# The routed token's feed-forward gets earlier keys in a planned order, and the planner's clock gets new times

## The chip, the cores and the metric

The kernel runs on one core of one Trainium2 chip. The metric is the device time of one execution in microseconds (us). TensorE is called PE here, VectorE DVE, ScalarE ACT, GpSimd POOL, and the engine whose queue issues every DMA is SP.

## The reference, cut to what matters

The kernel mixes two layers over the same 2048 tokens of 640 features: an attention with a compressive memory (32 heads of 20, four segments of 512 tokens), and a feed-forward for one routed token.

```python
g = _sigmoid((x * gate_w).sum(-1, keepdims=True))
# a: attention with memory, one segment of 512 tokens after the other
for s in range(N):
    p = _softmax(qs @ ks.T * scale + mask)
    a_dot = p @ vs
    a_mem = (phi(qs) @ M) / (phi(qs) @ z + 1e-6)
    o = sigmoid(beta) * a_mem + (1 - sigmoid(beta)) * a_dot
    M = M + phi(ks).T @ vs ; z = z + phi(ks).sum()
a = o @ wo
# b: x, plus the feed-forward at the token with the highest score r
r = x @ w_r
idx = argmax(r)
y = (silu(x[idx] @ w_gate) * (x[idx] @ w_up)) @ w_down * sigmoid(r[idx])
b = x.at[idx].add(y)
out = g * a + (1 - g) * b
```

## The kernel before

**How the order comes about.** The program does not issue its instructions as it writes them. Every piece of work is first entered into a plan with an engine (PE, ACT, DVE, POOL, SP), a duration in the planner's own clock, a key, and the buffers it reads and writes. `Plan.order` then plays the plan through: at each step it takes the engine whose best piece can start first, and among the pieces of that engine that can start at once (within 0.03 us) the one with the smallest key. The order that comes out is issued as it stands, and on the chip each engine works through its part in that order. A duration in the plan therefore never makes an instruction longer or shorter; it only decides what stands ahead of what. A DMA is two things in the plan: its issue on SP (0.36 us), and its landing, for which the planner adds 0.65 us, a time on 16 modelled rings, and 0.4 us.

**Keys.** The attention works in 32 groups `n` (4 heads of one segment). Group `n` has its score steps with row maxima under keys `n-1` to `n` (`a_step`, L792 and L798, the maxima at L804), its exponentials under `n` to `n+1` (`b_step`, L840 and L845), and its product with the values under `n+1` (`pv_step`, L866). One unit of the key is thus one group of heads. Projections of the next segment half (`paired`, L611, 64-row pairs) have keys around them, and so have the writes (L748) and reads (L729) of the memory.

**Modes on PE.** Pieces in mode "C" (L866, L729, L748 and the feed-forward, L967) use the array in 32-column strips; all others are in mode "R". The planner charges `SWITCH` for a change. A piece that is lazy (memory and feed-forward) is taken in mode C if its key is at most 1.0 above the smallest, and out of mode R only when its key is 1.0 behind all others that can start.

**The router and the feed-forward.** `route` (key 14.0) finds the token: `to_row` writes 128 maxima of 4 bytes each to DRAM (`rrow<-best`), reads them back as one row (`jp<-rrow`) and takes their maximum on DVE (L907); `to_all` sends it to all partitions (`sel<-top`, `all<-sel`). This is done twice, and then SP loads the token's row (`xrow`). The feed-forward has 18 up steps (`up_step`, keys 16.02 + 0.5 i), an activation (`ffn_act`, 25.0), 8 down steps (`down_step`, 25.6 + 0.3 i) and an end (`ffn_end`, 28.0), which leaves `yb`, the token's result on all partitions (POOL, L1025). A step loads one or two weight tiles into a ring of two (`ffn`), so the loads of the next step wait for the matmuls of this one.

**The output.** `o_job` makes one of 16 output tiles of 128 tokens: x is loaded, scaled (ACT, L1069), `yb` is added (DVE, L1070), 10 groups of six matmuls with `wo` follow (L611, 64x320), then L1081 adds the two and a DMA stores the tile. Twelve tiles (segments 0 to 2) have keys from 28.95 on and use three x buffers in the memory of `kk`; the last four have keys from 33.6. A PSUM pair is opened for a tile only when the work that its evacuation needs has been started in the plan:

```python
ps.guard = [d for u in ps.users if u.eng != "PE" for d in u.deps
            if d not in ps.users and d.eng != "PE"]
```

For an output tile this list holds L1070, and so the tile's matmuls stand behind `yb` in PE's order.

Of the kernel before, what the change touches and what calls it, by code (L numbers as in the profile page):

```python
# [112 lines left out]
class Plan:  # L113


    SWITCH = 0.2
    ISSUE = 0.36

    def __init__(self):
# [63 lines left out]
    def order(self):  # L183
# [86 lines left out]
        while len(done) < total:  # L270
            for e in stale:
                cur[e] = choose(e)
            stale = set()
            pick = None
            for e in ENGINES:
                c = cur[e]
                if c is not None and (pick is None or c[0] < pick[0]):
                    pick = c
            if pick is None:
                raise RuntimeError("the order is stuck: " + "; ".join(  # L280
                    f"{e}: {[(round(t.key, 2), t.seq, t.mode) for t in avail[e]][:6]}" for e in ENGINES))
            est, t = pick
            e = t.eng
            avail[e].remove(t)
            t.start = est
            know = seen[e]
            for d in t.deps:
                if d.eng != "PE":
                    know = max(know, d.seen)
                elif e != "PE":  # L290
                    know = max(know, d.index)
            if t.fence is not None:
                before, poke = t.fence
# [12 lines left out]
            t.fin = est + dur
            if t.desc is not None:
                count, size, wide = t.desc
                each = -(-count // wide) * (0.008 + size / 23400.0)
                begin, t.fin = t.fin + 0.65, 0.0  # L310
                for i in range(wide):
                    rings[i] = max(rings[i], begin) + each
                    t.fin = max(t.fin, rings[i] + 0.4)
            stale.add(e)
            if t.opens is not None:
                ps = t.opens
                if ps.need == 2:
# [40 lines left out]
def tile_infini_mod(  # L358
# [37 lines left out]

    banks = [psum.tile([128, 2, 512], F32, name=f"bank{i}") for i in range(PAIRS)]

    def dma(key, dst, src, reads, writes, desc, wide=16, issue=Plan.ISSUE):
        plan.add("SP", issue, lambda: nc.sync.dma_start(dst, src), key, reads, writes, desc=(*desc, wide))  # L400

    def dve(key, dur, fn, reads, writes):
        plan.add("DVE", dur, fn, key, reads, writes)
# [13 lines left out]
    def dves(n):  # L417
        return 0.13 + n / 940.0
# [7 lines left out]
    def split(key, engine, hi, lo, src, n, reads, hpart, lpart, more=0.0):  # L426

        act(key, acts(n) + 0.4 * more, lambda: nc.scalar.copy(hi, src), reads, [hpart])  # L428
        e, dur = (nc.gpsimd, pools(n) + 0.4 * more) if engine == "POOL" else (nc.vector, dves(n) + more)
        plan.add(engine, dur, lambda: e.tensor_tensor(out=lo, in0=src, in1=f32(hi), op=OP.subtract), key,  # L430
                 [*reads, hpart], [lpart])

# [288 lines left out]
    def memory_read(u, g, key):  # L721
# [7 lines left out]
                nc.tensor.matmul(t[32 * j:32 * j + 32, ps.bank, :], mbd.t[:, g, 32 * j:32 * j + 32], e.t, start=True, stop=True)  # L729
        pe(key, 0.9, fn, [(mbd, g), e], [ps], mode="C", opens=ps, lazy=True)  # L730
        nts[n] = nt = nt_ring.take()
        dve(key, dves(L), lambda: nc.vector.transpose(nt.t[:, 1, :], banks[ps.pair][:, ps.bank, :]), [ps], [(nt, 1)])
        z = sub(nt.t, L + DH, [[32, 16]])
        pool(key, 0.26, lambda: nc.gpsimd.tensor_scalar(z, z, 1e-6, None, op0=OP.add), [(nt, 1)], [(nt, 1)])

# [44 lines left out]
    def a_step(n, p, t, key):  # L780
# [7 lines left out]
        def fn():  # L788
# [6 lines left out]
            for w, other in ((tri, 0), (irt, 1)):  # L795
                for b in range(2):
                    dst = sub(a, 512 * b + at_ + 64 * (b ^ other), [[128, d], [1, 64]])
                    nc.tensor.matmul(dst, w.t[64 * b:64 * b + 64, :], sub(id64.t[64 * b:64 * b + 64], 0, [[0, d], [1, 64]]),  # L798
                                     start=False, stop=True, skip_group_check=True)
        dur = sum(stream(w) for _, _, w in blocks) + 2 * max(0.065, 0.03 * diag[1] + 0.01)  # L800
        pe(key, dur, fn, [(q, 0), (q, 1), (k, 0), (k, 1), tri, irt, id64], [ps], opens=ps)
        m_ = mxs[n]
        for i, at_, w in blocks:
# [48 lines left out]
    def pv_step(n, key):  # L852
# [14 lines left out]
                                     pt[j % 2, min(c, 2)].t[:, j // 2, at_:at_ + w], start=c == 0, stop=c == 3)  # L867
        pe(key, 2.2, fn, [*pt.values(), v], [ps], mode="C", opens=ps)
        nt = nts.pop(n) if n in nts else nt_ring.take()
        dve(key, dves(L), lambda: nc.vector.transpose(nt.t[:, 0, :], banks[ps.pair][:, ps.bank, :]), [ps], [(nt, 0)])  # L870
        norm(n, nt, key)

    def norm(n, nt, key):
# [10 lines left out]
        rd, rm = (sub(z.t, 16 * a, [[1, 16], [0, DH]]) for a in range(2))  # L884
        dve(key, dves(16 * DH), lambda: nc.vector.tensor_tensor(out=dot, in0=dot, in1=rd, op=OP.mult), [(nt, 0), z], [(nt, 0)])
        if s:
            pool(key, 1.15, lambda: nc.gpsimd.tensor_tensor(out=mem, in0=mem, in1=rm, op=OP.mult), [(nt, 1), z], [(nt, 1)])  # L887
            dve(key, 0.6, lambda: nc.vector.tensor_tensor(out=dot, in0=dot, in1=mem, op=OP.add), [(nt, 0), (nt, 1)], [(nt, 0)])
        dve(key, dves(L), lambda: nc.vector.transpose(o.t, nt.t[:, 0, :]), [(nt, 0)], [o])
        h = HH * hf + 4 * g  # L890
        dma(key, oT[32 * h:32 * h + 128, L * s:L * s + L], o.t, [o], [oTb[n]], (128, 2048))

# [7 lines left out]
    NT = S // 128  # L900

    def to_row(col, reads, k, key):
        dma(key, rrow[k].t.rearrange("o p -> p o"), col, reads, [rrow[k]], (128, 4))
        t = row
        dma(key, t.t, rrow[k].t, [rrow[k]], [t], (1, 512))
        m = buf(f"top{k}", [1, 1])
        dve(key, 0.25, lambda: nc.vector.tensor_reduce(out=m.t, in_=t.t, axis=AX.X, op=OP.max), [t], [m])  # L907
        return m

    def to_all(m, k, key):  # L910
        dma(key, sel[k].t, m.t, [m], [sel[k]], (1, 4))
        t = buf(f"all{k}", [128, 1])
        dma(key, t.t, bass.AP(tensor=sel[k].t.tensor, offset=sel[k].t.offset, ap=[[0, 128], [1, 1]]), [sel[k]], [t], (128, 4))
        return t

    def route():
# [25 lines left out]
        def load():  # L942
            i = nc.sync.value_load(ix.t[0:1, 0:1], min_val=0, max_val=S - 1)
            nc.sync.dma_start(xr.t, x[bass.ds(i, 1), :].rearrange("o (p t) -> (o p) t", t=KT))
        plan.add("SP", 1.2, load, key, [ix], [xr], desc=(128, 20, 16))
        R.update(gx=gx, gb=gb, oh=oh, sg=sg, xr=xr)

    at(14.0, route)
# [28 lines left out]
    def up_step(i):  # L977
# [2 lines left out]
        w = (wg, wu)[m].rearrange("(p t) f -> t p f", t=KT)  # L980
        parts = [(w[t, :, FP * f3:FP * f3 + FP], 128, [R["xr"]], lambda t=t: R["xr"].t[:, t:t + 1])
                 for t in range(2 * tt, min(2 * tt + 2, KT))]
        ffn_step(16.02 + 0.5 * i, fgu, FF // 4 * m + 144 * f3, 144, parts, tt == 0)

    for i in range(18):
        at(16.02 + 0.5 * i, lambda i=i: up_step(i))

    ht = buf("ht", [108, 2, 16])
    hv = buf("hv", [108, 16])

    def ffn_act():
# [11 lines left out]
        dve(key, 0.2, lambda: nc.vector.tensor_tensor(out=hv.t, in0=hv.t, in1=g_, op=OP.mult), [hv, (ht, 0)], [hv])  # L1003
        dve(key, 0.2, lambda: nc.vector.tensor_tensor(out=hv.t, in0=hv.t, in1=u_, op=OP.mult), [hv, (ht, 1)], [hv])

    at(25.0, ffn_act)
    ya = buf("ya", [128, YP])
    yb = Buf(fgu.t[:, :D], fgu)

    def down_step(i):  # L1010
        w = wd.rearrange("(p t) f -> t p f", t=16)
        parts = [(w[t], 108, [hv], lambda t=t: hv.t[:, t:t + 1]) for t in (2 * i, 2 * i + 1)]
        ffn_step(25.6 + 0.3 * i, ya, 0, YP, parts, i == 0)

    for i in range(8):
        at(25.6 + 0.3 * i, lambda i=i: down_step(i))

    def ffn_end():
        key = 28.0
        a = ya.t[0:1, :]  # L1020
        src = bass.AP(tensor=a.tensor, offset=a.offset, ap=[[a.ap[0][0] * 32, 4], [1, YP]])
        d = yrow.t
        dma(key, bass.AP(tensor=d.tensor, offset=d.offset, ap=[[YP, 4], [1, YP]]), src, [ya], [yrow], (4, 640))
        dma(key, yb.t, bass.AP(tensor=d.tensor, offset=d.offset, ap=[[0, 128], [1, D]]), [yrow], [yb], (128, 2560))
        pool(key, 1.5, lambda: nc.gpsimd.tensor_scalar(yb.t, yb.t, R["sg"].t, None, op0=OP.mult), [yb, R["sg"]], [yb])  # L1025

    at(28.0, ffn_end)

# [160 lines left out]
```

## Time and profile before

| | before |
|---|---|
| median of 3 runs | 681.44 us (681.03 to 681.76) |
| the profiled execution, its own time | 678.01 us |
| its span, first to last instruction | 676.3 us |
| mean granted TensorE clock | 0.955 of full speed |
| PE busy | 589.7 us (87%) |
| DVE, ACT, POOL busy | 435.1, 342.6, 295.3 us |
| DMA | 119.49 MB, mean 177 GB/s |

The rows of the trace are of the profiled execution. Its own time is 1.7 us above its span and 3.4 us below the median.

### The profile page before, as it was taken

How to read it: one execution, taken by the hardware profiler on the slowest of the kernel's cores; microseconds unless marked ns; L12 is line 12 of the kernel's file. 1: busy time of each engine (PE TensorE's matmuls, PEld its weight loads, DVE VectorE, ACT ScalarE, POOL GpSimd, SP SyncE). 2: the span in 40 equal slices, each digit the busy share in tenths (PEclk: the TensorE clock that was granted, in tenths of full speed). 3: DMA queues.
4: the chain of work that ended last, by engine and by line, in shares of the span. 5: the costliest groups of instructions: out<-in, count | busy, mean ns of one | idle time of the engine just before them, and what ended most of it. 6: DMA issues, size and time to landing. Idle time of an engine off the chain costs nothing.

```text
span 676.3 us, 18951 instructions
## 1 busy us (share of the span) xinstructions
PE 589.7 (87%) x7760; PEld 437.3 (65%) x7760; DVE 435.1 (64%) x783; ACT 342.6 (51%) x590; POOL 295.3 (44%) x408
## 2 busy tenths in 40 slices
PE   5989998998899867869899999988998787998886
PEld 2777765676667634546678765765676543687886
DVE  6767757776777675356867667666786757554332
ACT  7744764665475544536466655664445751340310
POOL 8953335443654463313633254435343742432310
PEclk9999999999999977979999999999998987799899
DMA  7577564543545444157757666567477554256422
GB/s 259 194 259 245 194 177 156 172 170 122 160 144 187 150 133 127 48 177 257 205 179 224 196 206 214 192 195 212 157 252 243 157 190 135 75 178 210 138 98 79
DMA packets 55943, 119.49 MB, mean 177 GB/s; under 512 B 6994, under 2 KB 10608, under 8 KB 55856
## 3 DMA queue, kind: packets, MB, share of 16 engines
q1 hardware_dynamic: 55856, 118.28, 54.4%
q8 instruction: 61, 1.00, 0.7%
q14 instruction: 26, 0.21, 0.1%
HBM read 72.62 MB, written 45.11 MB: 174 GB/s over the span
## 4 chain that ended last, share of the span: by engine, by line
PE 52%; DVE 18%; DMA 17%; issue 4%; SPq 3%; ACT 3%; POOL 2%; DVEq 0%; ACTq 0%; POOLq 0%
PE bank L611 24%; PE bank L866 10%; DVE mx L804 6%; PE bank L840 5%; PE bank L792 4%; SPq L400 3%; PE bank L729 3%; DMA rrow<-best 2%; DMA qs<-mr 2%; DVE nt L870 2%; DMA ffn<-in_wu_dram 2%; DMA kk<-in_x_dram 2%; PE bank L967 2%; DMA pb<-in_wc_dram 2%; PE bank L798 2%
## 5 line engine op out<-in xcount | busy, mean ns | idle before, releaser
L804 DVE TENSOR_REDUCE mx<-bank 128x2 f32<-128x1024 f32 (+3 forms) x256 | 199.1, 817 | 38.6 <-PE bank L798 35.4
L845 ACT ACTIVATE pb<-bank 128x768 f32<-128x768 f32 x128 | 101.8, 811 | 64.6 <-PE bank L840 49.7
L845 ACT ACTIVATE pa<-bank 128x1024 f32<-128x1024 f32 x64 | 65.7, 1026 | 93.9 <-PE bank L840 71.6
L847 POOL TENSOR_SCALAR_AFFINE_SELECT pb<-pb 128x256 f32<-128x256 f32 (+1 forms) x128 | 72.3, 568 | 88.5 <-ACT pb L845 86.7
L611 PE MATMUL bank<-xhi,whi 64*128 64x512 f32 (+1 forms) x480 | 100.8, 402 | 7.5 <-ACT whi L428 6.3
L792 PE MATMUL bank<-ks,qs 60*128 60x512 f32 (+3 forms) x512 | 79.4, 339 | 24.9 <-DVE mx L804 9.9
L840 PE MATMUL bank<-qs,ks 62*128 62x512 f32 (+3 forms) x512 | 81.0, 369 | 16.1 <-DVE mx L804 5.4
L611 PE MATMUL bank<-xhi,wlo 64*128 64x512 f32 (+1 forms) x480 | 90.9, 361 | 2.1 <-POOL wlo L430 1.1
L430 POOL TENSOR_TENSOR xlo<-raw,xhi 128x512 fp32r<-128x512 f32 x53 | 69.7, 1336 | 48.3 <-ACT xhi L428 29.8
L611 PE MATMUL bank<-xlo,whi 64*128 64x512 f32 (+1 forms) x480 | 90.3, 358 | 0.0
L792 PEld LDWEIGHTS bank<-ks,qs 60*128 60x128 f32 x512 | 49.3, 188 | 38.9 <-DVE mx L804 14.2
L840 PEld LDWEIGHTS bank<-qs,ks 62*128 62x128 f32 x512 | 47.8, 193 | 39.5 <-DVE mx L804 9.1
L870 DVE STREAM_TRANSPOSE nt<-bank 128x512 f32<-128x512 f32 x32 | 22.8, 713 | 67.3 <-PE bank L967 20.5
L430 POOL TENSOR_TENSOR lo<-xs,hi 128x512 fp32r<-128x512 f32 x40 | 52.2, 1321 | 31.3 <-ACT hi L428 19.9
L611 PEld LDWEIGHTS bank<-xhi,whi 64*128 64x128 f32 x480 | 49.8, 191 | 17.7 <-ACT whi L428 6.6
L611 PE MATMUL bank<-whi,xhi 64*128 64x320 f32 x320 | 51.3, 316 | 8.4 <-DVE nil L599 8.4
L611 PE MATMUL bank<-vhi,xhi 64*128 64x322 f32 x320 | 57.5, 339 | 0.6 <-DVE mx L804 0.6
L866 PEld LDWEIGHTS bank<-pb,va 128*32 128x32 f32 x768 | 27.7, 118 | 41.5 <-issue 36.9
L887 POOL TENSOR_TENSOR nt<-nt,zr 128x320 f32<-128x320 f32 x24 | 24.0, 999 | 69.8 <-DVE zr L881 68.9
L611 PEld LDWEIGHTS bank<-xhi,wlo 64*128 64x128 f32 x480 | 49.7, 190 | 6.6 <-POOL wlo L430 2.8
L847 POOL TENSOR_SCALAR_AFFINE_SELECT pa<-pa 128x256 f32<-128x256 f32 x64 | 28.9, 452 | 56.9 <-ACT pa L845 55.4
L611 PEld LDWEIGHTS bank<-xlo,whi 64*128 64x128 f32 x480 | 49.4, 188 | 5.7
(127 smaller groups left out, 1242.8 us busy)
## 6 DMA issues: line engine op xcount, KB each, us to landing
stk<-hi SPq DMA_DIRECT2D x40, 512.0 KB
qs<-stk SPq DMA_DIRECT2D x64, 240.0 KB
ks<-stk SPq DMA_DIRECT2D x64, 240.0 KB
stk<-lo SPq DMA_DIRECT2D x40, 256.0 KB
raw<-in_xT_dram SPq DMA_DIRECT2D x35, 256.0 KB
oT<-on SPq DMA_DIRECT2D x32, 256.0 KB
ffn<-in_wg_dram SPq DMA_DIRECT2D x15, 288.0 KB
ffn<-in_wu_dram SPq DMA_DIRECT2D x15, 288.0 KB
```

The lines of the kernel that those rows point to most:

```text
L400: plan.add("SP", issue, lambda: nc.sync.dma_start(dst, src), key, reads, writes, desc=(*desc, wide))
L430: plan.add(engine, dur, lambda: e.tensor_tensor(out=lo, in0=src, in1=f32(hi), op=OP.subtract), key, [*reads, hpart], [lpart])
L611: nc.tensor.matmul(t[:, b, :n], w[64 * r:64 * r + 64], m[64 * r:64 * r + 64], start=i == 0 and p == 0, stop=ends and p == 2, skip_group_ch ...
L729: nc.tensor.matmul(t[32 * j:32 * j + 32, ps.bank, :], mbd.t[:, g, 32 * j:32 * j + 32], e.t, start=True, stop=True)
L792: nc.tensor.matmul(a[:, b, at_:at_ + w], q.t[64 * b:64 * b + ST, p, 128 * i:128 * i + 128], k.t[64 * b:64 * b + ST, p, :w], start=m == 0, ...
L804: dve(key - 0.6, 0.15 + 2 * w / 960.0, lambda i=i, at_=at_, w=w: nc.vector.tensor_reduce(out=m_.t[:, :, p, i], in_=banks[ps.pair][:, :, at ...
L840: nc.tensor.matmul(bt[:, b, at_:at_ + w], k.t[64 * b:64 * b + ST + 2, p, 128 * c:128 * c + 128], q.t[64 * b:64 * b + ST + 2, p, L - w:], s ...
L845: act(key - 0.4, 0.22 + 2 * w / 1270.0, lambda: nc.scalar.activation(pt.t, banks[ps.pair][:, :, :w], AF.Exp, scale=SCALE), [ps], [pt])
L847: pool(key, 0.42 if t < 2 else 0.64, lambda: nc.gpsimd.affine_select(out=d, in_=d, pattern=[[0, 2], [0, len(cs)], [1, 128]], base=0, chann ...
L866: nc.tensor.matmul(o[32 * j:32 * j + 32, ps.bank, L - w:], v.t[:, c, VW * h:VW * h + 32], pt[j % 2, min(c, 2)].t[:, j // 2, at_:at_ + w], ...
L870: dve(key, dves(L), lambda: nc.vector.transpose(nt.t[:, 0, :], banks[ps.pair][:, ps.bank, :]), [ps], [(nt, 0)])
L887: pool(key, 1.15, lambda: nc.gpsimd.tensor_tensor(out=mem, in0=mem, in1=rm, op=OP.mult), [(nt, 1), z], [(nt, 1)])
```

## The change

All of it is in the plan; no instruction is added, removed or given another shape. The feed-forward's keys become FIRST + UP i for the up steps (15.5 + 0.36 i, so 15.5 to 21.6), 22.0 for the activation, DOWN + 0.25 i for the down steps (22.5 to 24.25), and 24.7 for the end. Landings get an `extra`: 0.8 us for every load that reads only what was there at the start, 6.4 us for the write of the 128 maxima, 1.9 us for their reading back, 1.4 us for the two spreadings to all partitions, and 1.0 us for the token's row. Some durations and the charge for a mode change are set anew.

```diff
+FIRST, UP, DOWN = 15.5, 0.36, 22.5
-    SWITCH = 0.2
+    SWITCH = 0.1
-                count, size, wide = t.desc
+                count, size, wide, extra = t.desc
-                    t.fin = max(t.fin, rings[i] + 0.4)
+                    t.fin = max(t.fin, rings[i] + 0.4 + extra)
-    def dma(key, dst, src, reads, writes, desc, wide=16, issue=Plan.ISSUE):
+    def dma(key, dst, src, reads, writes, desc, wide=16, issue=Plan.ISSUE, extra=0.0):
+        if not reads:
+            extra = 0.8
...
-        e, dur = (nc.gpsimd, pools(n) + 0.4 * more) if engine == "POOL" else (nc.vector, dves(n) + more)
+        e, dur = (nc.gpsimd, pools(n) + 0.4 * more) if engine == "POOL" else (nc.vector, dves(n) + (0.0 if not more else -0.02))
...
-        dur = sum(stream(w) for _, _, w in blocks) + 2 * max(0.065, 0.03 * diag[1] + 0.01)
+        dur = sum(stream(w) for _, _, w in blocks) + 0.07
...
-            pool(key, 1.15, lambda: nc.gpsimd.tensor_tensor(out=mem, in0=mem, in1=rm, op=OP.mult), ...
-            dve(key, 0.6, lambda: nc.vector.tensor_tensor(out=dot, in0=dot, in1=mem, op=OP.add), ...
+            pool(key, 1.04, ...
+            dve(key, 0.49, ...
...
-        dma(key, rrow[k].t.rearrange("o p -> p o"), col, reads, [rrow[k]], (128, 4))
+        dma(key, rrow[k].t.rearrange("o p -> p o"), col, reads, [rrow[k]], (128, 4), extra=6.4)
-        dma(key, t.t, rrow[k].t, [rrow[k]], [t], (1, 512))
+        dma(key, t.t, rrow[k].t, [rrow[k]], [t], (1, 512), extra=1.9)
...
-        ffn_step(16.02 + 0.5 * i, fgu, FF // 4 * m + 144 * f3, 144, parts, tt == 0)
+        ffn_step(FIRST + UP * i, fgu, FF // 4 * m + 144 * f3, 144, parts, tt == 0)
-        key = 25.0
+        key = DOWN - 0.5
-        ffn_step(25.6 + 0.3 * i, ya, 0, YP, parts, i == 0)
+        ffn_step(DOWN + 0.25 * i, ya, 0, YP, parts, i == 0)
-        key = 28.0
+        key = DOWN + 2.2
```

Three transposes on DVE (L732, L870, L889) get 0.71 or 0.72 us for 0.67 us in the plan.

## Rows read from the trace of the kernel before

**Rows 1.** Windows: PE, PEld, DVE, ACT, POOL busy (instructions), PEclk, DMA share, GB/s.

```profile
240.00:300.00 60.00, 42.29 (x362) 26.41 (x358) 31.73 (x72) 24.10 (x57) 19.86 (x31) 0.78 0.35 109
300.00:500.00 200.00, 186.30 (x2694) 135.65 (x2694) 138.40 (x253) 115.07 (x190) 88.22 (x126) 1.00 0.66 206
...
533.00:584.00 51.00, 39.95 (x416) 20.85 (x406) 29.86 (x57) 20.82 (x30) 22.90 (x36) 0.77 0.48 152
584.00:651.00 67.00, 58.60 (x754) 55.19 (x752) 32.76 (x50) 20.40 (x29) 20.39 (x18) 0.97 0.49 162
651.00:676.30 25.30, 19.34 (x252) 18.46 (x252) 6.97 (x15) 2.19 (x4) 2.55 (x2) 0.94 0.18 66
```

**Rows 2.** Chain that ended last: start, us, what.

```profile
255.25 7.58 DMA rrow<-best
...
279.80 8.30 DMA rrow<-best
288.12 3.63 DMA jp<-rrow
...
671.68 0.88 DVE pb L1081
```

**Rows 3.** Timeline of PE, 260 to 294: in brackets idle before, releaser.

```profile
267.18 0.86 PE L792 MATMUL bank<-ks,qs 60*128 60x512 f32 x2 [3.99 <-DVE mx L804]
...
293.03 0.69 PE L792 MATMUL bank<-ks,qs 60*128 60x384 f32 x2 [6.81 <-DVE ix L929]
```

**Rows 4.** Timeline of DVE, 282 to 292.

```profile
291.77 0.27 DVE L907 TENSOR_REDUCE top<-jp 1x1 f32<-1x128 f32 x1 [8.33 <-DMA jp<-rrow]
```

**Rows 5.** Timeline of PE, 305 to 575: feed-forward (L967) and two value products (L866).

```profile
305.82 1.06 PE L866 MATMUL bank<-pa,va 128*32 128x512 f32 x8
...
314.93 0.70 PE L967 MATMUL bank<-ffn,xrow 128*32 128x144 f32 x16
...
478.38 1.06 PE L866 MATMUL bank<-pa,va 128*32 128x512 f32 x8
...
485.17 0.45 PE L967 MATMUL bank<-ffn,xrow 128*32 128x144 f32 x8
...
498.84 0.73 PE L967 MATMUL bank<-ffn,hv 108*32 108x160 f32 x16
...
507.94 0.48 PE L967 MATMUL bank<-ffn,hv 108*32 108x160 f32 x8 [1.59 <-DMA ffn<-in_wd_dram]
...
531.83 0.75 PE L967 MATMUL bank<-ffn,hv 108*32 108x160 f32 x16
...
563.96 0.75 PE L967 MATMUL bank<-ffn,hv 108*32 108x160 f32 x16
...
568.87 1.49 PE L967 MATMUL bank<-ffn,hv 108*32 108x160 f32 x16
...
574.65 1.29 PE L967 MATMUL bank<-ffn,hv 108*32 108x160 f32 x16
```

**Rows 6.** Timeline of PE, 463.9 to 464.6: one step between pairs.

```profile
463.96 0.31 PE L611 MATMUL bank<-vhi,xlo 64*128 64x322 f32 x2
464.20 0.45 PE L967 MATMUL bank<-ffn,xrow 128*32 128x144 f32 x8
464.58 0.41 PE L611 MATMUL bank<-vhi,xhi 64*128 64x322 f32 x2
```

**Rows 7.** Timelines of POOL, DVE and PE, 534 to 585.

```profile
534.12 2.49 POOL L430 TENSOR_TENSOR xlo<-raw,xhi 128x512 fp32r<-128x512 f32 x2
...
581.70 1.89 POOL L1025 TENSOR_SCALAR fgu<-fgu,sg 128x640 f32<-128x640 f32 x1 [2.81 <-DMA fgu<-yrow]
...
583.72 2.60 DVE L1070 SCALAR_TENSOR_TENSOR kk<-fgu,oh,kk 128x640 f32<-128x640 f32 x3
...
584.22 0.34 PE L611 MATMUL bank<-whi,xhi 64*128 64x320 f32 x2
```

**Rows 8.** Waits of SP's queue, 300 to 584: us in total, times, longest.

```profile
SPq L400 <- PE bank L967: 28.0, 19, 4.8
```

More of the change, by code (lines that the diff above doesn't have):

```diff
@@ L397, in tile_infini_mod @@
     banks = [psum.tile([128, 2, 512], F32, name=f"bank{i}") for i in range(PAIRS)]
-    def dma(key, dst, src, reads, writes, desc, wide=16, issue=Plan.ISSUE):
-        plan.add("SP", issue, lambda: nc.sync.dma_start(dst, src), key, reads, writes, desc=(*desc, wide))
+    def dma(key, dst, src, reads, writes, desc, wide=16, issue=Plan.ISSUE, extra=0.0):
+        if not reads:
+            extra = 0.8
+        plan.add("SP", issue, lambda: nc.sync.dma_start(dst, src), key, reads, writes, desc=(*desc, wide, extra))
     def dve(key, dur, fn, reads, writes):
@@ L731, in memory_read @@
         nts[n] = nt = nt_ring.take()
-        dve(key, dves(L), lambda: nc.vector.transpose(nt.t[:, 1, :], banks[ps.pair][:, ps.bank, :]), [ps], [(nt, 1)])
+        dve(key, 0.71, lambda: nc.vector.transpose(nt.t[:, 1, :], banks[ps.pair][:, ps.bank, :]), [ps], [(nt, 1)])
         z = sub(nt.t, L + DH, [[32, 16]])
@@ L869, in pv_step @@
         nt = nts.pop(n) if n in nts else nt_ring.take()
-        dve(key, dves(L), lambda: nc.vector.transpose(nt.t[:, 0, :], banks[ps.pair][:, ps.bank, :]), [ps], [(nt, 0)])
+        dve(key, 0.72, lambda: nc.vector.transpose(nt.t[:, 0, :], banks[ps.pair][:, ps.bank, :]), [ps], [(nt, 0)])
         norm(n, nt, key)
@@ L886, in norm @@
         if s:
-            pool(key, 1.15, lambda: nc.gpsimd.tensor_tensor(out=mem, in0=mem, in1=rm, op=OP.mult), [(nt, 1), z], [(nt, 1)])
-            dve(key, 0.6, lambda: nc.vector.tensor_tensor(out=dot, in0=dot, in1=mem, op=OP.add), [(nt, 0), (nt, 1)], [(nt, 0)])
-        dve(key, dves(L), lambda: nc.vector.transpose(o.t, nt.t[:, 0, :]), [(nt, 0)], [o])
+            pool(key, 1.04, lambda: nc.gpsimd.tensor_tensor(out=mem, in0=mem, in1=rm, op=OP.mult), [(nt, 1), z], [(nt, 1)])
+            dve(key, 0.49, lambda: nc.vector.tensor_tensor(out=dot, in0=dot, in1=mem, op=OP.add), [(nt, 0), (nt, 1)], [(nt, 0)])
+        dve(key, 0.71, lambda: nc.vector.transpose(o.t, nt.t[:, 0, :]), [(nt, 0)], [o])
         h = HH * hf + 4 * g
@@ L912, in to_all @@
         t = buf(f"all{k}", [128, 1])
-        dma(key, t.t, bass.AP(tensor=sel[k].t.tensor, offset=sel[k].t.offset, ap=[[0, 128], [1, 1]]), [sel[k]], [t], (128, 4))
+        dma(key, t.t, bass.AP(tensor=sel[k].t.tensor, offset=sel[k].t.offset, ap=[[0, 128], [1, 1]]), [sel[k]], [t], (128, 4), extra=1.4)
         return t
@@ L944, in load @@
             nc.sync.dma_start(xr.t, x[bass.ds(i, 1), :].rearrange("o (p t) -> (o p) t", t=KT))
-        plan.add("SP", 1.2, load, key, [ix], [xr], desc=(128, 20, 16))
+        plan.add("SP", 1.2, load, key, [ix], [xr], desc=(128, 20, 16, 1.0))
         R.update(gx=gx, gb=gb, oh=oh, sg=sg, xr=xr)
@@ L982, in up_step @@
                  for t in range(2 * tt, min(2 * tt + 2, KT))]
-        ffn_step(16.02 + 0.5 * i, fgu, FF // 4 * m + 144 * f3, 144, parts, tt == 0)
+        ffn_step(FIRST + UP * i, fgu, FF // 4 * m + 144 * f3, 144, parts, tt == 0)
     for i in range(18):
-        at(16.02 + 0.5 * i, lambda i=i: up_step(i))
+        at(FIRST + UP * i, lambda i=i: up_step(i))
     ht = buf("ht", [108, 2, 16])
@@ L1004, in ffn_act @@
         dve(key, 0.2, lambda: nc.vector.tensor_tensor(out=hv.t, in0=hv.t, in1=u_, op=OP.mult), [hv, (ht, 1)], [hv])
-    at(25.0, ffn_act)
+    at(DOWN - 0.5, ffn_act)
     ya = buf("ya", [128, YP])
@@ L1012, in down_step @@
         parts = [(w[t], 108, [hv], lambda t=t: hv.t[:, t:t + 1]) for t in (2 * i, 2 * i + 1)]
-        ffn_step(25.6 + 0.3 * i, ya, 0, YP, parts, i == 0)
+        ffn_step(DOWN + 0.25 * i, ya, 0, YP, parts, i == 0)
     for i in range(8):
-        at(25.6 + 0.3 * i, lambda i=i: down_step(i))
+        at(DOWN + 0.25 * i, lambda i=i: down_step(i))
     def ffn_end():
-        key = 28.0
+        key = DOWN + 2.2
         a = ya.t[0:1, :]
@@ L1023, in ffn_end @@
         dma(key, bass.AP(tensor=d.tensor, offset=d.offset, ap=[[YP, 4], [1, YP]]), src, [ya], [yrow], (4, 640))
-        dma(key, yb.t, bass.AP(tensor=d.tensor, offset=d.offset, ap=[[0, 128], [1, D]]), [yrow], [yb], (128, 2560))
+        dma(key, yb.t, bass.AP(tensor=d.tensor, offset=d.offset, ap=[[0, 128], [1, D]]), [yrow], [yb], (128, 2560), extra=1.4)
         pool(key, 1.5, lambda: nc.gpsimd.tensor_scalar(yb.t, yb.t, R["sg"].t, None, op0=OP.mult), [yb, R["sg"]], [yb])
-    at(28.0, ffn_end)
+    at(DOWN + 2.2, ffn_end)
     WALL = ("qa", "ka", "qb", "kb")
```

## The prediction, as it was put on record

> **What bounds the kernel now.** I read the windows first. From 300 to 500 PE is busy 186.3 of 200 us at full clock [rows 1]: that is how dense PE can be here, 0.93. Two stretches fall far short of it. From 240 to 300 PE is busy 42.3 of 60 us at a mean clock of 0.78, and from 533 to 584 it is busy 39.95 of 51 us at 0.77 [rows 1]. In both no other engine comes near PE's busy time, so neither is bound by an engine; something is waited for. The chain and the timelines say for what.
>
> In the first stretch it is the router. The chain runs through two writes of the 128 maxima, 7.58 and 8.30 us to landing, and a reading back of 3.63 us [rows 2]. The planner prices such a write at about 1.1 us behind its issue (0.65 + 0.4 and nearly nothing on the rings). It therefore puts the reading back right behind the write on SP, and the maximum (L907) soon after on DVE. On the chip SP stands at the read until the write lands, and all that is behind it in SP's queue stands too: weight tiles, row maxima, spills. DVE stands 8.33 us at the second L907 [rows 4] with maxima of score blocks behind it, and PE waits 3.99 and 6.81 us for just those [rows 3].
>
> In the second stretch it is the feed-forward. The operands of the first four output tiles are ready when POOL ends its last split at 534.12 + 2.49 = 536.6; the token's result is started at 581.70, takes 1.89 us, DVE adds it at 583.72, and the first output matmul runs at 584.22 [rows 7]. Since the plan opens no PSUM pair before L1070 is placed, no output matmul can stand earlier in PE's queue. For 47.6 us twelve tiles' work is held back while PE idles a fifth of the time at the lower clock in part.
>
> **The change, step by step.** No instruction is added or removed, so what can change is the order alone.
>
> *Router.* The write now costs 7.5 us in the plan (1.1 + 6.4) against 7.58 and 8.30 on the chip [rows 2], the reading back about 3.0 against 3.63. The planner will put other DMAs between write and read, and other maxima ahead of L907. The chain of the router itself stays as long as it is; what goes are the waits of those behind it. Floor: 0, if something else binds there at once. Ceiling: the stretch's work at full clock is 42.29 x 0.78 = 33.0 us (busy time times granted clock, an approximation), at a density of 0.93 35.5 us, so 24.5 of the 60 us. I take the two named waits of PE, 3.99 + 6.81 = 10.8 us [rows 3], and leave the half-clock work behind them in the range. What is late next is the row's load, and with it the first up step, which has room.
>
> *Pace of the feed-forward.* Today the up steps run from 314.93 to 485.17, 170.2 us for 17 gaps, 10.0 us each, and the down steps from 498.84 to 574.65 with a gap from 507.94 to 531.83 [rows 5]. One unit of the key is (478.38 - 305.82)/11 = 15.7 us, these being the value products of groups 13 and 24 [rows 5], so a spacing of 0.5 asks for 7.8 us and the steps slip behind their keys: a lazy step waits for the next piece in mode C. The new spacing 0.36 asks for 5.65 us. The steps then fall behind their keys faster, and from a lag of 1.0 the planner takes them anywhere, also between the matmuls of mode R; then only the loads limit them. How fast that can be is seen from 563.96 to 568.87 and to 574.65: 4.9 and 5.8 us [rows 5]. So the pace lies between 5.8 and 10.0 us; I take 7.5. The first step moves by about half a unit, to 306. Then: 17 x 7.5 = 127 to 433; 13.7 us for the activation, as from 485.17 to 498.84; 7 x 7.5 = 53 to 500; and 583.6 - 574.65 = 8.9 us for the end: `yb` at 509. At 5.8 us it would be at 468, at the old paces at 306 + 170 + 14 + 76 + 9 = 575. What counts is whether `yb` comes before 536.6, when the tiles' operands are there; that needs a mean pace of (536.6 - 306 - 22.6)/24 = 8.7 us, so 7.5 has room.
>
> *What the early result is worth.* From 533 on PE's work at full clock is 39.95 x 0.77 + 58.60 x 0.97 + 19.34 x 0.94 = 30.8 + 56.8 + 18.2 = 105.8 us [rows 1]. With output tiles to fill the gaps of the last attention groups, as projections fill them from 300 to 500, 105.8/0.93 = 113.8 us, to 646.8; then 676.3 - 671.68 = 4.6 us for the last evacuation and store [rows 2]: an end at 651.4, 24.9 us earlier. About 2 us of that lie before 536.6, so 23. Floor: 0 if the tiles only displace attention and leave the same holes at the end; ceiling 24.9. I take 23, because the last four tiles depend on group 31 and other tiles' work is then left to cover their loads, as now.
>
> *What it costs.* Steps that stand alone change the mode twice. A lone step begins 0.24 us after the start of the pair ahead of it [rows 6], and that pair itself fills some of this; so a change costs between 0 and 0.24 us, 26 steps with two changes at most 12.5 us. Many steps stand alone today too, as this one. I take 2 us. The Trainium skill, "TensorEngine Tiling (Array Packing)", section Tiling Modes, Key Properties, says that a change of tiling mode drains the TensorE. Read at its hardest, the step would not begin before the pair ends, 463.96 + 0.31 = 464.27; the trace has it begin at 464.20, so a full drain is not seen in these modelled ends, and an estimate by that page, 0.31 us for each of 52 changes, would put 16 us in place of my 2 and the forecast at 664.
>
> *The rest.* The 0.8 us on first loads, the transposes, the 1.04 and 0.49 us in the norm and the 0.07 us in the score steps shift many pieces by tenths of a microsecond in the plan. Their landings are hidden behind PE work wherever it is dense; where it isn't they could gain or lose. I price them at 0 with 3 us on either side, somewhat under the smaller of the two waits [rows 3].
>
> **Sum.** -23 - 10.8 + 2 = -31.8 us. The span of 676.3 becomes 644.5, the profiled execution's own time 678.0 becomes 646.2. The median of the runs is 3.4 us above that execution: 649.6, so 650.
>
> **Rivals.**
>
> *The pace stays.* The steps keep waiting for mode C, and the feed-forward ends at 575. For it: the 10.0 us per step with loads long there, and a gap of 24 us among the down steps, when a late key did not help [rows 5]. Against: today's keys are mostly less than a unit late, the new ones will be more. Worth of the early result (584.2 - 575)/47.6 x 23 = 4.4 us: 681.4 - 4.4 - 10.8 + 2 = 668; half-way, with `yb` at 542, 42/47.6 x 23 = 20 and 652.
>
> *Router without a gain.* The waits move to another engine, since the chain stays as long: 681.4 - 23 + 2 = 660. For it: PE has only 33.0 us of work in that stretch, and the new weights' splits fall there too. Against: the two waits have one cause each.
>
> *Slower: PE stands in front of weight tiles.* A step placed between other matmuls blocks PE until its tiles land, if the plan has the landing too early; at 507.94 that was 1.59 us [rows 5]. And SP waits 28.0 us in 19 times, up to 4.8 us, for these steps before it can load into the ring of two [rows 8], with row maxima and spills behind it. Closer steps do both more often. If each of the 26 cost 1.59 us, that is 41 us: 681.4 - 31.8 + 41 = 691. From 31.8/26 = 1.2 us per step it decides. Against: the plan's landings get later by 0.8 us, which makes such waits rarer.
>
> *Nothing comes of it.* The order near the end and at the router changes, and other waits of equal size take over: 681.
>
> **Chances.** Both gains, near 650: 0.52. The pace stays wholly or in part, 652 to 668: 0.22. No gain at the router, 660: 0.12. Slower: 0.10. No change: 0.04. A measurement of this kernel tells about 0.2% from nothing. Faster by more than that is then 0.52 + 0.22 + 0.12 = 0.86, within it 0.04, slower 0.10. The low end takes both ceilings nearly whole: 681.4 - 24.9 - 24.5 = 632, so 634. The high end takes in the first two rivals and 4 us: 672. The likeliest case alone, with the router between half and one and a half times its value and the result between 17 and 25 us, lies between 642 and 661.
>
> **What would show it.** Right: no PE wait of several microseconds between 240 and 300, and clock near 1.00 there; L907 without a long wait on DVE; up steps under 9 us apart; L1025 before 540; the first 64x320 matmuls at about 530, among L840 and L792; PE near 0.93 from there to the end. Wrong: L1025 after 560; or an early `yb` and yet holes of PE behind the last value product, waiting for `raw<-oT` splits; or PE idle in front of L967 for more than a microsecond each.

## The result, and the profile after

The changed kernel takes 649.97 us (median of 4 runs, 647.77 to 650.81) against 681.24 us (679.31 to 681.76, 4 runs) for the kernel before: a ratio of 0.9541, 95% interval 0.9510 to 0.9572. The profiled execution took 650.81 us, its span 649.1, mean granted clock 0.981 against 0.955. Medians are over all executions here, while ratios and their intervals leave out those classed as slow, so the two need not agree. The kernel before was run 39 more times beside the experiments, with times from 675.1 to 688.9 us: a spread of about a percent either way, not the 0.2% that I had counted on. In the new program every line number from L611 on is three higher (L907 is L910, L967 is L970, L1025 is L1028), and SP's issues are L403. One thing besides the order differs, against what I wrote: `Plan.order` drops a small copy of DVE (L599, now L602) where the order makes it needless, and 46 of them are left of 52.

The windows, to be laid beside [rows 1] (same columns; the last stretch ends earlier now):

```profile
240.00:300.00 60.00, 49.44 (x478) 33.92 (x478) 38.38 (x77) 31.08 (x68) 23.86 (x35) 0.84 0.66 151
300.00:500.00 200.00, 186.37 (x2735) 133.59 (x2734) 137.36 (x255) 105.83 (x176) 86.11 (x124) 1.00 0.67 210
...
533.00:584.00 51.00, 46.46 (x594) 35.73 (x594) 37.23 (x60) 21.16 (x31) 26.61 (x35) 1.00 0.48 152
584.00:625.00 41.00, 36.04 (x462) 31.15 (x462) 21.55 (x34) 18.89 (x27) 13.95 (x17) 1.00 0.56 182
625.00:649.10 24.10, 18.52 (x250) 18.00 (x246) 6.93 (x15) 1.84 (x4) 2.55 (x2) 0.97 0.18 70
```

PE is busier in the router's stretch (49.4 of 60 us, 42.3 before), the same from 300 to 500, and busy 46.5 of 51 us at full clock where it had 39.95 at 0.77.

The router, on the timeline of SP between 250 and 305:

```profile
255.66 0.33 SPq L403 DMA_DIRECT2D rrow<-best  x1
257.28 0.62 SPq L403 DMA_DIRECT2D qs<-mr  x1
...
270.29 0.42 SPq L403 DMA_DIRECT2D jp<-rrow  x1
...
284.75 0.53 SPq L403 DMA_DIRECT2D rrow<-best  x1
286.62 0.69 SPq L403 DMA_DIRECT2D qs<-mr  x1
...
301.45 0.29 SPq L403 DMA_DIRECT2D jp<-rrow  x1
```

and on that of DVE:

```profile
275.15 0.27 DVE L910 TENSOR_REDUCE top<-jp 1x1 f32<-1x128 f32 x1
...
308.93 0.26 DVE L910 TENSOR_REDUCE top<-jp 1x1 f32<-1x128 f32 x1
```

The reading back now stands 14.6 and 16.7 us behind its write, with other DMAs between them, and the maximum has no bracket: DVE did not idle right before it, where it had stood 8.33 us [rows 4]. The price is a router that takes longer, its second maximum at 308.93. What PE still waits for in that stretch is the landing of new weights and of a spill:

```profile
258.84 8.10 DMA raw<-in_wc_dram
...
268.82 1.10 PE bank L843 x6
...
283.96 6.07 DMA ks<-stk
290.17 0.23 PE bank L795
```

These are lines of the chain. The waits of PE that end at 268.82 and 290.17 are 2.88 and 1.76 us, against 3.99 and 6.81 before [rows 3].

The feed-forward on the timeline of PE (first and last up step, first down step, and the two halves of the last, which waited for each of its two tiles):

```profile
321.67 0.70 PE L970 MATMUL bank<-ffn,xrow 128*32 128x144 f32 x16
...
447.51 0.43 PE L970 MATMUL bank<-ffn,xrow 128*32 128x144 f32 x8
456.38 0.75 PE L970 MATMUL bank<-ffn,hv 108*32 108x160 f32 x16 [0.39 <-ACT xhi L431]
...
508.74 0.48 PE L970 MATMUL bank<-ffn,hv 108*32 108x160 f32 x8 [0.62 <-DMA ffn<-in_wd_dram]
...
511.09 0.69 PE L970 MATMUL bank<-ffn,hv 108*32 108x160 f32 x8 [1.87 <-DMA ffn<-in_wd_dram]
```

From start to start that is (447.51 - 321.67)/17 = 7.4 us per up step and (508.74 - 456.38)/7 = 7.5 per down step. Then its end, on the timelines of SP, POOL and PE:

```profile
512.55 0.57 SPq L403 DMA_DIRECT2D yrow<-ya  x1
...
519.77 0.41 SPq L403 DMA_DIRECT2D raw<-oT  x1
520.23 0.41 SPq L403 DMA_DIRECT2D fgu<-yrow  x1
...
529.60 1.89 POOL L1028 TENSOR_SCALAR fgu<-fgu,sg 128x640 f32<-128x640 f32 x1
...
533.35 0.31 PE L614 MATMUL bank<-whi,xhi 64*128 64x320 f32 x2
```

`yb` is there at 531.5 in place of 583.6, and the first output matmul runs at 533.35 in place of 584.22 [rows 7].

### The profile page after: what moved, and what is told of

The parts are those of the page before. It is cut to its first block, busy times and chain, and to the rows that moved or that the text cites. A ratio compares the mean times of both kernels' runs of the same rounds, so it can differ in the third digit from the quotient of the medians.

```text
span 649.1 us, 18950 instructions
## 1 busy us (share of the span) xinstructions
PE 581.8 (90%) x7760; PEld 435.5 (67%) x7760; DVE 440.2 (68%) x777; ACT 342.9 (53%) x590; POOL 294.5 (45%) x408
## 4 chain that ended last, share of the span: by engine, by line
PE 33%; DMA 17%; DVE 5%; ACT 3%; SPq 3%; issue 2%; POOL 1%; ACTq 0%; DVEq 0%; POOLq 0%
PE bank L614 16%; PE bank L869 5%; PE bank L843 3%; SPq L403 3%; PE bank L795 2%; DMA ffn<-in_wu_dram 2%; DMA qs<-mr 2%; PE bank L970 2%; PE bank L732 2%; DMA ffn<-in_wd_dram 2%; DMA out_dram<-kk 2%; DMA kk<-in_x_dram 2%; DMA raw<-oT 1%; ACT pb L848 1%; DVE mx L807 1%
## 5 line engine op out<-in xcount | busy, mean ns | idle before, releaser
L614 PE MATMUL bank<-xhi,whi 64*128 64x512 f32 (+1 forms) x480 | 102.4, 399 | 6.6 <-ACT whi L431 6.3
L614 PE MATMUL bank<-xhi,wlo 64*128 64x512 f32 (+1 forms) x480 | 94.5, 367 | 1.6 <-DVE wlo L433 1.3
L843 PE MATMUL bank<-qs,ks 62*128 62x512 f32 (+3 forms) x512 | 81.9, 361 | 14.6 <-DMA qs<-mr 4.7
L614 PE MATMUL bank<-xlo,whi 64*128 64x512 f32 (+1 forms) x480 | 93.4, 363 | 0.0
L795 PE MATMUL bank<-ks,qs 60*128 60x512 f32 (+3 forms) x512 | 79.0, 336 | 11.3 <-DVE mx L807 2.5
L433 POOL TENSOR_TENSOR xlo<-raw,xhi 128x512 fp32r<-128x512 f32 x53 | 68.3, 1308 | 37.3 <-ACT xhi L431 34.6
L614 PEld LDWEIGHTS bank<-xhi,whi 64*128 64x128 f32 x480 | 52.5, 194 | 14.2 <-ACT whi L431 6.3
L614 PE MATMUL bank<-vhi,xhi 64*128 64x322 f32 x320 | 59.6, 340 | 1.1 <-DVE nt L735 1.1
L614 PEld LDWEIGHTS bank<-xhi,wlo 64*128 64x128 f32 x480 | 52.3, 192 | 8.1 <-DVE wlo L433 3.4
L614 PEld LDWEIGHTS bank<-xlo,whi 64*128 64x128 f32 x480 | 52.1, 191 | 6.3
L614 PE MATMUL bank<-vlo,xhi 64*128 64x322 f32 x320 | 55.3, 313 | 0.0
L614 PE MATMUL bank<-vhi,xlo 64*128 64x322 f32 x320 | 55.3, 313 | 0.0
```

Of the source, the lines that this page charges most:

```text
L614: nc.tensor.matmul(t[:, b, :n], w[64 * r:64 * r + 64], m[64 * r:64 * r + 64], start=i == 0 and p == 0, stop=ends and p == 2, skip_group_ch ...
L795: nc.tensor.matmul(a[:, b, at_:at_ + w], q.t[64 * b:64 * b + ST, p, 128 * i:128 * i + 128], k.t[64 * b:64 * b + ST, p, :w], start=m == 0, ...
L843: nc.tensor.matmul(bt[:, b, at_:at_ + w], k.t[64 * b:64 * b + ST + 2, p, 128 * c:128 * c + 128], q.t[64 * b:64 * b + ST + 2, p, L - w:], s ...
```

## The experiments

Two theories stood against each other once the single parts had run. A: the parts have effects of their own, some needing each other, and their sum is the 31 us. B: each edit reshuffles the whole order, and a good part of the 31 us belongs to this one order and to no part.

In the tables, "V" is the end of the last projection of values, "yb" the end of L1025 (L1028), "out" the first output matmul, "end" the span, all in us from the profiles. "Won" is work that PE has done more than in the kernel before in that stretch: busy time times granted clock, from windows of 10 us. Over the whole span that product is 566.8 to 574.7 us in the fourteen profiles, though the work is the same, so differences of 3 or 4 us are no reading. And each row is one execution: that of keys_only took 679.13 us, 4.3 over its median, that of no_keys 666.43, 4.9 under.

| kernel | V | yb | out | end | won 240-300 | 300-520 | 520-640 |
|---|---|---|---|---|---|---|---|
| before | 528.2 | 583.6 | 584.2 | 676.3 | 0 | 0 | 0 |
| after | 522.3 | 531.5 | 533.4 | 649.1 | 8.7 | -0.6 | 18.7 |
| keys_only | 550.4 | 518.9 | 550.2 | 677.4 | 0.3 | -4.8 | 10.3 |
| router_only | 527.3 | 591.6 | 589.9 | 683.4 | 6.5 | -0.9 | -8.1 |
| loads_only | 535.7 | 596.7 | 591.6 | 687.7 | -3.3 | -3.9 | -1.7 |
| durations_only | 516.1 | 592.9 | 589.6 | 684.3 | 7.3 | -4.1 | -9.1 |
| no_keys | 506.3 | 581.0 | 576.2 | 664.7 | 9.2 | 4.6 | -2.5 |
| no_router | 532.3 | 531.0 | 540.2 | 670.6 | 5.4 | -7.7 | 8.2 |
| no_loads | 531.2 | 533.8 | 535.6 | 674.9 | 4.1 | -8.2 | 7.1 |
| no_durations | 548.6 | 525.6 | 545.7 | 671.6 | 5.7 | -11.5 | 13.1 |
| nudge_dve | 526.7 | 525.5 | 533.2 | 661.3 | 5.8 | -3.4 | 11.5 |
| nudge_act | 532.5 | 556.0 | 556.1 | 669.1 | 10.9 | -12.8 | 12.8 |
| nudge_before | 532.6 | 589.8 | 586.0 | 679.4 | 0.6 | -0.5 | -0.5 |
| gate_open | 524.7 | 589.3 | 525.9 | 669.1 | 0.2 | 1.1 | 5.0 |

### One part alone

**keys_only**: the kernel before with the new keys and nothing else.

```diff
-        ffn_step(16.02 + 0.5 * i, ...)      # up; ffn_act at 25.0
-        ffn_step(25.6 + 0.3 * i, ...)       # down; ffn_end at 28.0
+        ffn_step(FIRST + UP * i, ...)       # 15.5 + 0.36 i; 22.0
+        ffn_step(DOWN + 0.25 * i, ...)      # 22.5 + 0.25 i; 24.7
```

> The kernel before with the new keys of the feed-forward alone; clock and prices as before. Theory of two gates (the result yb gates the output tiles, the router's waits gate the rest): the output gate is opened, so 658 to 666 us, that is 681.2 less 15 to 23; yb before 545, and PE near 0.93 at full clock from there; between 240 and 300 the two waits behind L907 stay (PE about 42 of 60 us). Rival, that the new prices are what makes the order good: the keys alone give under 5 us, 676 or more.

Measured: 674.88 us, ratio 0.9931 (0.9893 to 0.9970). `yb` comes at 518.9, earlier still than in the changed kernel, and only 5 us are gained, near what the rival named and far from the 658 to 666 us of the theory. The router's stretch is as it was, with waits of 5.41 and 7.87 us before L910:

```profile
269.05 0.27 DVE L910 TENSOR_REDUCE top<-jp 1x1 f32<-1x128 f32 x1 [5.41 <-DMA jp<-rrow]
294.34 0.27 DVE L910 TENSOR_REDUCE top<-jp 1x1 f32<-1x128 f32 x1 [7.87 <-DMA jp<-rrow]
```

PE has 4.8 us less done between 300 and 520, the projections of values end 22 us later, and the output starts only when they do, at 550. With `yb` early, what comes last for an output tile is its own operands: SP issues the first of their loads (`raw<-oT`) at 538.58, where it was 516.63 before and 511.11 in the changed kernel, and POOL's split of them ends just ahead of the first output matmul. Timelines of POOL and PE:

```profile
548.79 1.27 POOL L433 TENSOR_TENSOR xlo<-raw,xhi 128x512 fp32r<-128x512 f32 x1 [11.19 <-DMA raw<-oT]
...
550.17 0.47 PE L614 MATMUL bank<-whi,xhi 64*128 64x320 f32 x2
```

**router_only**: the kernel before with the longer landings of the router, the token's row and `yb`.

```diff
-        dma(key, rrow[k].t..., col, reads, [rrow[k]], (128, 4))
-        dma(key, t.t, rrow[k].t, [rrow[k]], [t], (1, 512))
+        dma(key, rrow[k].t..., col, reads, [rrow[k]], (128, 4), extra=6.4)
+        dma(key, t.t, rrow[k].t, [rrow[k]], [t], (1, 512), extra=1.9)
...
+        ...   # in words: extra=1.4 for all<-sel and for yb, 1.0 for xrow
```

> The kernel before with the later landings of the router's DMAs, the token's row and yb's spreading alone. Theory of two gates: 670 to 674 us (8 to 11 less), all of it between 240 and 300, where no wait behind L907 is left; yb still near 575, and the hole before it as before. Rival, that the waits only move to another engine: 678 to 684, with PE still near 42 of 60 us in that stretch.

Measured: 687.25 us, ratio 1.0133 (1.0075 to 1.0192): slower, and above both ranges named ahead. The router's part works, 45.2 us of PE in place of 42.3 and a value product of group 13 at 300.7 in place of 305.8:

```profile
240.00:300.00 60.00, 45.16 (x450) 30.06 (x451) 36.56 (x79) 29.99 (x69) 23.97 (x36) 0.85 0.52 142
...
533.00:584.00 51.00, 41.41 (x396) 20.87 (x396) 29.71 (x58) 23.90 (x34) 20.48 (x33) 0.72 0.54 164
```

But `yb` comes at 591.6, 8 us later than before, and the stretch before it is as thin as it was, at a clock of 0.72. What was won at the router is lost again ahead of the output.

**loads_only** and **durations_only**: the kernel before with the 0.8 us on DMAs that read no tile, and with the new durations and `SWITCH`.

```diff
+        if not reads:
+            extra = 0.8
```

```diff
-    SWITCH = 0.2
+    SWITCH = 0.1
...
-            pool(key, 1.15, ...)   # and 0.6; transposes dves(L)
+            pool(key, 1.04, ...)   # and 0.49; transposes 0.71, 0.72; split and L798 as in the change
```

> The kernel before with 0.8 us more on every load that reads only what was there at the start. Theory of two gates: within 3 us of 681. Rival, that this price makes the order good: 672 or less. Third possibility, that any small edit of the clock scatters the order: several us either way, with no one place in the trace that it comes from.

> The kernel before with the mode change at 0.1 us and the new durations (splits, transposes, norm, score steps) alone. Theory of two gates: within 3 us of 681. Rival, that the clock makes the order good: 672 or less. Third possibility, scatter of the order: several us either way.

Measured: 691.57 us, ratio 1.0172 (1.0096 to 1.0247), and 684.54 us, ratio 1.0024 (0.9980 to 1.0068). The first is slower beyond its interval, as only the third possibility allowed; the second can't be told from no change. In both `yb` comes later, at 596.7 and 592.9. The span ends 91.0 and 91.4 us behind it, 91.8 in router_only and 92.7 before. With the old keys the end follows `yb` nearly rigidly, whatever was won ahead of it (durations_only had the value product of group 13 at 293.1, 12.7 us earlier than before). The last order with the old keys, no_keys below, is shorter there: 83.7 us, in an execution 4.9 us under its median.

The four parts alone change the median by -5.4, +6.9, +11.3 and +4.2 us of the 680.32 that the kernel before had beside them; the ratio of durations_only, 1.0024, doesn't bear out the last. Together they bring -31.

### The change without one part

Each is the changed kernel with the edits of one part, as shown above, taken back.

> The changed kernel with the old keys of the feed-forward, all new prices kept. Theory of the gate (the four runs before this one with old keys all end 91 to 93 us after yb is ready): yb at 580 to 592 again, and the end 91 to 93 us behind it, so 677 to 690 us, with the router's gain lost. Rival, scatter of the order: anywhere from 650 to 690, not tied to yb.

> The changed kernel with the old landings of the router's DMAs and of yb's spreading, all else new. Theory of the gate: yb is early, so the end hangs on PE's work, and the router's waits of about 8 us count again: 656 to 662. Rival, that the router's waits are swallowed here too: within 3 us of 650. Scatter: 665 or more, with the loss outside 240 to 300.

> The changed kernel without the 0.8 us on first loads. Theory that this price is what keeps PE from standing in front of the feed-forward's tiles: PE's waits for ffn tiles rise from what they are in the changed kernel towards the 5.8 us of the kernel with the new keys alone, and the time is 655 to 668. Rival, that it was the router's and not the loads' price that the keys lacked: within 3 us of 650.

> The changed kernel with the old durations and the mode change at 0.2 us. Theory of the gate: within 4 us of 650, since yb stays early. Rival, that the durations decide how densely the late part is packed: 660 or more, with yb early all the same and PE under 0.9 behind it.

Measured, against 678.34 us before: no_keys 671.33, ratio 0.9886 (0.9832 to 0.9941); no_router 671.81, 0.9901 (0.9859 to 0.9943); no_loads 675.77, 0.9952 (0.9908 to 0.9995); no_durations 673.64, 0.9933 (0.9893 to 0.9974). Whichever part is taken away, by the medians 21 to 26 us of the gain go with it, and four parts cannot each own two thirds of it. The changed kernel was not run again beside these or the nudges below; by the ratios, each to the kernel before run beside it, 23 to 28 us go.

no_keys is faster than the 677 to 690 us that the gate alone asked for. no_router has a time named for scatter (665 or more), no_durations one named by its rival (660 or more), and no_loads lies above the 655 to 668 of its theory.

no_keys is the one that can be read: denser than all others up to 520, then the closed gate.

```profile
300.00:500.00 200.00, 190.38 (x2785) 140.98 (x2785) 145.57 (x266) 113.16 (x188) 89.77 (x127) 1.00 0.66 207
...
533.00:584.00 51.00, 42.05 (x440) 24.38 (x440) 26.52 (x54) 19.84 (x27) 17.77 (x29) 0.78 0.44 139
```

The other three have `yb` at 526 to 534, as the changed kernel has, and lose 8 to 12 us of PE's work between 300 and 520. Waits for weight tiles don't explain that. PE's waits on `ffn` tiles between 300 and 520 are 6.0 us in the changed kernel, 7.1 and 7.3 in no_router and no_loads, and 4.3 in no_durations, which lost most there:

```profile
L970 PE MATMUL bank<-ffn,xrow 128*32 128x144 f32 x240 | 11.4, 292 | 3.4 <-DMA ffn<-in_wu_dram 1.7 <-DMA ffn<-in_wg_dram 1.3 <-ACT pb L848 0.2
...
L970 PE MATMUL bank<-ffn,hv 108*32 108x160 f32 x128 | 6.6, 313 | 3.4 <-DMA ffn<-in_wd_dram 3.0 <-ACT xhi L431 0.4
```

Those are the groups by line of the changed kernel between 300 and 520 (idle time ahead of the group, by what ended it, last); and those of no_durations:

```profile
L970 PE MATMUL bank<-ffn,xrow 128*32 128x144 f32 x240 | 12.1, 302 | 4.1 <-DMA ffn<-in_wg_dram 2.7 <-ACT pa L848 1.0 <-DVE zr L884 0.4
...
L970 PE MATMUL bank<-ffn,hv 108*32 108x160 f32 x128 | 6.4, 306 | 2.0 <-DMA ffn<-in_wd_dram 1.6 <-DVE mx L807 0.4
```

### Edits that say nothing, and the gate by itself

**nudge_dve**, **nudge_act**, **nudge_before**: if theory A holds, an edit of a thousandth of a microsecond in the planner's clock should leave the time alone; if B holds, it costs what an edit of a whole part costs. The first two are made in the changed kernel, the third is the edit of nudge_act made in the kernel before. The expected texts call theory A the theory of a cause and B the lucky order, or scatter.

```diff
-        return 0.13 + n / 940.0     # dves, a DVE duration
+        return 0.131 + n / 940.0
```

```diff
-        return 0.2 + n / 1250.0     # acts, an ACT duration
+        return 0.199 + n / 1250.0
```

> The changed kernel with a price that says nothing new: every DVE duration that goes by size 0.001 us longer. The order comes out otherwise in places. Theory that the four parts are needed together for a cause (an early result that is priced as the chip has it): within 6 us of 650. Rival, that the changed kernel is a lucky order, and any edit costs the 21 to 26 us that each of the four removals cost: 665 to 675.

> The changed kernel with every ACT duration that goes by size 0.001 us shorter, again a price that says nothing new. Theory of a cause: within 8 us of 650. Rival, lucky order: 665 to 675.

> The kernel before with every ACT duration that goes by size 0.001 us shorter. Theory of the gate: the end stays 91 to 93 us behind yb, and yb within some us of 584, so 675 to 688. Rival, scatter: 20 us or more from 681 either way.

Measured, against 680.11 us before: nudge_dve 663.72, ratio 0.9783 (0.9694 to 0.9871); nudge_act 668.84, 0.9816 (0.9745 to 0.9887); nudge_before 680.71, 1.0032 (0.9998 to 1.0065). By the medians the nudges cost the changed kernel 14 and 19 us (16 and 19 by the ratios), the kernel before 0.6. nudge_dve falls between the two ranges named ahead, nudge_act into that of the lucky order, nudge_before into that of the gate. In the windows of nudge_act most of the loss lies between 300 and 500, where the changed kernel has 186.37 us at full clock:

```profile
300.00:500.00 200.00, 179.41 (x2504) 126.69 (x2502) 129.01 (x243) 101.68 (x167) 81.59 (x116) 0.95 0.65 196
```

and its `yb` comes at 556.0. In nudge_dve `yb` (525.5) and the first output (533.2) are as early as in the changed kernel or earlier, and the loss is spread thinly, 3, 3 and 7 us in the three stretches of the table, too little in any one to be placed. By these two draws theory B is right for 14 to 19 of the 31 us, and what two arbitrary orders of the same change keep is about 2%.

**gate_open**: is the gate alone worth that? The kernel before, in which L1070 takes x in place of `yb` and so waits for nothing of the feed-forward; the routed token's result is left out of its output.

```diff
-            out=xf, in0=yb.t, scalar=R["oh"].t[:, i:i + 1], in1=xf, ...), [xb, yb, R["oh"]], [xb])
+            out=xf, in0=xf, scalar=R["oh"].t[:, i:i + 1], in1=xf, ...), [xb, R["oh"]], [xb])
```

> The kernel before with one operand changed: the instruction that adds yb to an output tile reads x in yb's place, so the routed token's result is left out of the output; the instruction stays, the feed-forward runs as before, and nothing of the output waits for it any more. Theory of the gate: output tiles start as soon as their operands are there, at 530 to 545 in place of 584, and the time is 655 to 668, since the router's waits stay. Rival, that an early start of the tiles alone is worth little, as in the kernel with the new keys alone: 672 or more.

Measured: 669.65 us, ratio 0.9819 (0.9735 to 0.9903), 10.5 us faster with the old router and the old keys, between the 655 to 668 of the theory and the 672 of its rival. The first output matmul and the windows:

```profile
525.89 0.41 PE L611 MATMUL bank<-whi,xhi 64*128 64x320 f32 x2
```

```profile
533.00:584.00 51.00, 45.41 (x565) 30.21 (x564) 28.57 (x53) 21.47 (x29) 19.27 (x29) 0.90 0.56 172
584.00:640.00 56.00, 46.48 (x566) 38.85 (x566) 30.02 (x50) 21.16 (x31) 23.57 (x25) 0.95 0.53 165
```

The held-back tiles fill the stretch from 533 (45.4 us at 0.90 in place of 39.95 at 0.77), though not to a density of 0.93: behind 584 it is 46.48/56 = 0.83.

None of the twelve beats the changed kernel.

## Why the prediction was right, and where it was not

The forecast of 650 us met 649.97. The gate that carried it is shown, the router's share of it is not, and that the number fits so well is partly chance.

**The gate: shown.** L1070 holds back twelve tiles, and an early `yb` lets them go. gate_open shows it without any other edit, and the old-key orders show it from the other side, five of them with an end 90 to 93 us behind `yb` and one with 84. It is a gate of the plan's order more than a wait on the chip: in five of these six orders the first output matmul runs 1.7 to 5.1 us before `yb` is there.

**The pace: right.** 7.4 and 7.5 us per step against 7.5 assumed. The first step came at 322, not 306, behind the later second maximum; the activation took 8.9 us, not 13.7; the last down step began at 509, not 500. The end of the feed-forward took 22.8 us from there to 531.5, not the 8.9 copied from the old order. There SP went straight from `yrow` to its reading back; now it has ten DMAs between the two (7.7 us), and POOL has its own queue ahead of L1028. `yb` came at 531.5, not 509. That cost little, because it was still ahead of the bound that counted, 536.6.

**The router: half right.** The two long waits went, and PE did 8.7 us more work in that stretch against the 10.8 of waits. The clock did not come near 1.00 as I had said: it is 0.84, since PE still stands for landings there. And how much of the 8.7 us is the router's isn't shown. durations_only has the old landings, and DVE stands there as before, yet PE does 7.3 us more in that stretch than in the kernel before:

```profile
265.23 0.27 DVE L910 TENSOR_REDUCE top<-jp 1x1 f32<-1x128 f32 x1 [6.58 <-DMA jp<-rrow]
...
281.87 0.27 DVE L910 TENSOR_REDUCE top<-jp 1x1 f32<-1x128 f32 x1 [5.52 <-DMA jp<-rrow]
```

no_router, where these waits sum to 10.2 us, keeps 5.4 of the 8.7. Nor has the term a worth of its own, which the sum didn't say: router_only is 7 us slower, with a `yb` 8 us later and, the gate being closed, an end that moves with it.

**The worth of the early result: the term that was mis-sized.** The sum has 23 us, from all the work behind 533 at a density of 0.93. gate_open has 10.5 by the medians and 12.3 by the ratio (interval 6.6 to 18.0), for tiles that start even 7 us earlier than in the changed kernel. In the changed kernel the same reckoning gives 46.46 x 1.00 + 36.04 x 1.00 + 18.52 x 0.97 = 100.5 us of work in 116.1 us, 0.87 in place of 0.74 before (105.8 in 143.3). 105.8 us at 0.87 take 122 us, 21 us less, where the sum's reckoning had 24.9 and took 23 of it; the table, by windows of 10 us, has 18.7 behind 520. The orders of the nudges got 11.5 and 12.8 there.

**"The rest", priced at 0 with 3 us on either side: the step that failed.** I took an edit of the planner's clock for a shift of tenths of a microsecond that dense work hides. On this plan it is a new order everywhere. Of its own two parts loads_only moved the time by +11.3 us and durations_only, by its ratio, by less than the 3; 0.001 us moved that of the changed kernel by 14 and 19. With the gate closed the spread shows as the time of `yb` (581.0 to 596.7 over six orders); with the new keys, as PE's work done between 300 and 520 (-0.6 to -12.8 us). The three orders of the whole change lie at 650, 664 and 669 us, and the four that keep its early feed-forward without one or more of the other parts at 672 to 676. Had I known no more than that, 664 would have been the forecast; it is inside the range given, but not its middle.

**The rivals.** PE in front of weight tiles: 6.0 us of such waits in all over 26 steps, 0.23 us each, far under the 1.2 that decides; SP's waits for PE before it can load the ring are as before, to be laid beside [rows 8]:

```profile
SPq L403 <- PE bank L970: 27.9, 19, 5.0
```

The pace that stays is refuted in this order. The router without a gain is refuted for the stretch, where more work was done, but not as to the cause, as said above. Nothing comes of it: not here, though no_loads, with three of the four parts, comes near it (0.9952).

**Open.** Why the other orders with an early feed-forward lose 3 to 13 us between 300 and 520, and this one next to nothing, isn't settled. It isn't waits on weight tiles alone: in nudge_act these are 7.3 us, 1.3 more than in the changed kernel, and its other waits there, on splits, spills and row maxima, are 1 to 3 us each in sum. I found no single cause. Nor does any run tell apart the 2 us that the sum has for changes of mode. With two nudges, 14 and 19 us are two draws and not a spread, and how much of the 2% that they keep belongs to the keys and how much to the router is not told apart either: no_router and keys_only are single orders too.

## What to carry to other kernels

In a kernel whose order comes from a greedy plan, look for the piece that gates the tail and measure "end minus gate" over several orders: where it is constant, as 90 to 93 us here, nothing won ahead of the gate counts until the gate moves. Before crediting a gain to a part of such a change, nudge the plan by an amount that means nothing; here that alone moved the time by 14 and 19 us, more than any part taken by itself. Nudge the changed kernel and not only the one before: the edit that cost the one 19 us moved the other by 0.6. A forecast of a change of order should carry that spread as a term of its own, and a good order is worth keeping as a list, since the next harmless edit may lose it.

## What the runs showed of the hardware that I had not expected

The two writes of 128 times 4 bytes took 7.58 and 8.30 us to landing before [rows 2] and 7.38 and 7.71 in gate_open; with those on the chains of loads_only, durations_only and no_router, ten writes in five orders took 6.86 to 8.59 us, where the planner had 1.1. And the granted clock stays under full speed in windows in which PE hardly idles, after windows in which it did; means as these are a mix of its two levels, 1.2 and 2.4 GHz. In the windows of the changed kernel, 10 us each (columns as in [rows 1]):

```profile
260.00:270.00 10.00, 5.86 (x54) 4.16 (x52) 5.16 (x12) 3.15 (x7) 1.57 (x3) 0.94 0.59 109
270.00:280.00 10.00, 10.00 (x103) 6.57 (x103) 6.57 (x12) 7.27 (x13) 5.03 (x6) 0.89 0.50 179
280.00:290.00 10.00, 7.56 (x102) 6.57 (x98) 5.59 (x13) 6.73 (x14) 5.89 (x8) 0.97 0.87 181
290.00:300.00 10.00, 9.83 (x99) 6.97 (x99) 3.90 (x6) 4.69 (x8) 0.96 (x2) 0.69 0.98 150
```

So a wait costs twice here, once as idle time and again as slower matmuls behind it. On the timeline of PE, right behind the wait that ends at 268.82 and 3 us later, two pairs of one size:

```profile
269.72 0.63 PE L614 MATMUL bank<-xhi,whi 64*128 64x512 f32 x2
...
273.12 0.39 PE L614 MATMUL bank<-xlo,whi 64*128 64x512 f32 x2
```
